# Attention and two MLPs in one kernel: TensorE's filler and score matmuls are queued behind the transposes of earlier slots

## The chip, the cores and the metric

The kernel runs on one core of one Trainium2 chip. The metric is the device time of one execution in microseconds (us); before the change the median of three runs is 1144.47 us (1142.77 to 1144.97).

## What is computed

Multi-head attention over 4 batches, 12 heads, 448 tokens and a head size of 64, with RMS-normalised queries and keys, and behind it two MLPs without biases:

```python
def _attn_ref(q, k, v, g_q, g_k):
    q_n, k_n = rmsnorm(q, g_q), rmsnorm(k, g_k)
    scores = scale * np.matmul(q_n, k_n.transpose(0, 1, 3, 2))
    scores = scores - np.max(scores, axis=-1, keepdims=True)
    attn = np.exp(scores)
    attn = attn / (np.sum(attn, axis=-1, keepdims=True) + 1e-09)
    return np.matmul(attn, v)

def _moe_ref(x, w1, w2, w3, w_out):        # 1792 tokens, 768 -> 1024 -> 768
    return ((x @ w1) * (x @ w2) @ w3) @ w_out

def _moe2_ref(x, w_in, w_out):             # 1792 tokens, 768 -> 2048 -> 768
    h = x @ w_in
    return (h * np.clip(h + 3.0, 0.0, 6.0) / 6.0) @ w_out
```

## The kernel before

**Stages.** The 48 heads are worked off as 24 pairs, numbered 0 to 23 here. A pair takes eight *slots*; a slot is one block of 112 queries of one head against all 448 keys. `attention` (L470) loops over the slots `t` (L875 to L902). While attention runs, TensorE also does *filler*: first the product of `w3` and `w_out` (`wprime`, L252), then layer 1 and layer 2 of the first MLP for the batches whose attention is finished (L391 and L396, L88 to L90). `fill` (L439) hands out some microseconds of filler per slot. When the slots are used up, at about 617 us, the rest of the filler runs alone; from about 705 us on the second MLP runs (L1242, L1304).

**One slot.** `score` (L618) makes the scores with two matmuls (L627, L628) into a bank of accumulator memory. VectorE scales them, finds the row maximum (L634) and negates it (L641); ScalarE takes the exponential (L646). Eight slots later `trans` (L649) turns the result in four small matmuls (L653). ScalarE copies the turned block out as `xh` (L662; for the block that two heads share L664 and L665), VectorE makes the remainder `xl` (L672; L674 and L675), and `pv` multiplies both with the values (L705 and L706; L696, L693 for the shared block). The turned blocks and the scores have two banks each.

**The round trip of a pair.** When the row sums of a pair are complete, TensorE turns them (L561; a second small one, L564, in every other pair), VectorE copies them (L578), one transfer takes them to DRAM (`rsd`), two bring them back spread over 64 partitions each (`rsb`), GpSimd multiplies the result of the pair with them (L730), and ScalarE splits that product for layer 1 (L359). I call the time from L561 to the end of L730 the round trip.

**What sets the order.** The kernel is written slot by slot, but a scheduler orders each engine's instructions when the program is built. `tc.issue_after(x)` around a block makes each instruction of that block that runs on `x`'s engine stand behind `x` in that engine's queue; it adds no wait at run time. Before the change the filler of slot `t` stands behind the scores, the maximum and the exponential of a slot two or three back (`anchors`, L897). At run time every engine works off its queue in order, and an instruction that waits holds up all that stands behind it.

Of the kernel before, what the change touches and what calls it, by code (L numbers as in the profile page):

```python
# [26 lines left out]
P = 128  # L27
CP = 112
# [22 lines left out]
def fused_kernel(ctx: ExitStack, tc: tile.TileContext, nat, qT, kT, vin, gq, gk,  # L51
                 w12, w3t, wo, win, wo2, outT):
    nc = tc.nc
# [16 lines left out]
    ident = cpool.tile([P, P], F32, name="ident")  # L70
# [21 lines left out]
    def bank(tag, name="bank"):  # L92
        return pp.tile([P, 512], F32, tag=tag, name=name)
# [12 lines left out]
    now = [0]  # L106
# [7 lines left out]
    def run_tasks():  # L114
        for fn, a in tasks.pop(now[0], ()):
            fn(*a)
# [322 lines left out]
    def fill(us, aux):  # L439

        state["aux"] = min(state["aux"] + aux, 2 * aux)
        while state["aux"] > 0 and prep[0] is not None:
            c = prep[0].step()
            if c is None:
                break
            state["aux"] -= c
        state["early"] = min(state["early"] + 0.6, 1.2)
        while state["early"] > 0 and "early" in L:
            c = next(L["early"], None)
            if c is None:  # L450
                break
            state["early"] -= c
        state["debt"] = min(state["debt"] + us, 2 * us)
        while state["debt"] > 0 and not state["done"]:
            try:
                c = next(filler)
            except StopIteration:
                state["done"] = True
                return
            if c is None:  # L460
                return
            state["debt"] -= c
            if "pool" in L:
                state["spent"] += c


    T = {}
    anchors = {}

    def attention(ap, rate):  # L470
        def full(i):
            return i in FULL
# [145 lines left out]
        def score(i, s):  # L618
            j, c = divmod(s, NC)
            if s == 0:  # L620
                T["PP", i] = ap.tile([CP, NC, 2 * S], F32, tag="PP", bufs=2, name="PP")
                T["m", i] = ap.tile([CP, 16], F32, tag="mx", bufs=2, name="mx")
                T["sum", i] = ap.tile([CP, 8], F32, tag="sum", bufs=2, name="sum")
            k1, k2 = T["K", i]
            ps = bank("s")
            qs = T["Q", i][:, j, c * CP : c * CP + CP]
            nc.tensor.matmul(ps[:CP, :S], qs, k1[:, j, :], start=True, stop=False)  # L627
            anchors[8 * i + s] = [nc.tensor.matmul(ps[:CP, :S], qs, k2[:, j, :], start=False, stop=True)]  # L628
            return ps

        def scale_max(i, s, ps):
            j, c = divmod(s, NC)
            sl = slice(j * S, j * S + S)
            anchors[8 * i + s].append(nc.vector.tensor_tensor_reduce(  # L634
                out=T["PP", i][:, c, sl], in0=ps[:CP, :S], in1=T["rb", i][:, sl],
                op0=ALU.mult, op1=ALU.max, scale=T["rq", i][:, s : s + 1], scalar=-3e38,
                accum_out=T["m", i][:, s : s + 1]))

        def negate(i, s):
            m = T["m", i]  # L640
            nc.vector.tensor_scalar_mul(m[:, 8 + s : 9 + s], m[:, s : s + 1], -1.0)  # L641

        def expo(i, s):
            j, c = divmod(s, NC)
            v = T["PP", i][:, c, j * S : j * S + S]
            anchors[8 * i + s].append(nc.scalar.activation(  # L646
                v, v, AF.Exp, bias=T["m", i][:, 8 + s : 9 + s], accum_out=T["sum", i][:, s : s + 1]))

        def trans(i, kb):  # L649
            src = T["PP", i]  # L650
            ps = bank("t")
            for c in range(NC):
                nc.tensor.transpose(ps[:, c * CP : c * CP + CP], src[:, c, kb * P : kb * P + P],  # L653
                                    ident[:CP, :CP])
            hi = ap.tile([P, S], F32 if full(i) else F32R, tag="xh", bufs=3, name="xh")
            lo = None if full(i) else ap.tile([P, S], F32R, tag="xl", bufs=3, name="xl")
            T["X", i, kb] = (ps[:, :S], hi, lo)

        def thi(i, kb):
            ps, hi, lo = T["X", i, kb]  # L660
            if kb != 3 or i < K3 or full(i):
                nc.scalar.activation(hi, ps, AF.Copy)  # L662
            else:
                nc.scalar.activation(hi[0:64, :], ps[0:64, :], AF.Copy)  # L664
                nc.scalar.activation(lo[64:128, :], ps[64:128, :], AF.Copy)  # L665

        def tlo(i, kb):
            ps, hi, lo = T["X", i, kb]
            if full(i):
                return  # L670
            if kb != 3 or i < K3:
                nc.vector.tensor_sub(lo, ps, hi)  # L672
            else:
                nc.vector.tensor_sub(hi[64:128, :], ps[0:64, :], hi[0:64, :])  # L674
                nc.vector.tensor_sub(lo[0:64, :], ps[64:128, :], lo[64:128, :])  # L675
# [57 lines left out]
        def xnext():  # L733
            for i in sorted(xs_ready)[: 2]:
                if len(L["xhl"]) < XB:
                    xsplit(i)
# [77 lines left out]
        ps = bank("t")  # L814
# [11 lines left out]
        for i in range(NP):  # L826
            t = 8 * i
# [46 lines left out]
        t = -1  # L874
        while t < 8 * NP + 23 or xs_ready:  # L875
            t += 1
            if t == 4:
                first.close()
            now[0] = t
            live = t < 8 * NP  # L880
            ps = score(*divmod(t, 8)) if live else None
            if 0 < t <= 8 * NP:
                expo(*divmod(t - 1, 8))
            u = t - LG
            if 0 <= u < 8 * NP and u % 8 < 7:
                trans(*divmod(u, 8))
            if 0 <= u - 1 < 8 * NP and (u - 1) % 8 < 7:
                tlo(*divmod(u - 1, 8))
            if live:
                scale_max(t // 8, t % 8, ps)  # L890
                negate(*divmod(t, 8))
            if 0 <= u < 8 * NP and u % 8 < 7:
                thi(*divmod(u, 8))
            if 0 <= u - 2 < 8 * NP and (u - 2) % 8 < 7:
                pv(*divmod(u - 2, 8))
            with ExitStack() as es:
                for a in anchors.get(t - (3 if "pool" in L else 2), ()):  # L897
                    es.enter_context(tc.issue_after(a.ins))
                fill(*rate(t))
            run_tasks()  # L900
            if "pool" in L:
                xnext()  # L902

    def rate(t):
        if "pool" not in L:
            return 1.3, 3
        if L["cur"] < 8:
            return 2.5, 4
        left = (B - 1) * (2 * M1 * KD * 3 + KD * M1 * 3) * 0.189 - state["spent"]
        return max(left - 25.0, 0.0) / max(8 * NP + 14 - t, 1), 2  # L910
# [508 lines left out]
```

## Time and profile before

| | |
|---|---|
| median of three runs | 1144.47 us (1142.77 to 1144.97) |
| the profiled execution's own time | 1141.81 us |
| its span, first to last instruction | 1140.0 us |
| TensorE busy | 1103.1 us, 97% of the span, 5483 matmuls |
| weight loads of TensorE | 944.0 us, 83% |
| VectorE busy | 850.8 us, 75% |
| ScalarE busy | 812.4 us, 71% |
| GpSimd busy | 177.9 us, 16% |
| DMA | 299.04 MB, mean 262 GB/s |
| granted TensorE clock, mean | 0.998 |

In the rows below PE is TensorE's matmuls, PEld its weight loads, DVE VectorE, ACT ScalarE, POOL GpSimd and SP the engine whose queue issues the transfers. Matmuls overlap: a matmul of 448 columns is shown as 0.36 us long, yet the next one starts 0.2 us after it. So idle time that stands in brackets on a PE row counts from the end of the drawn bar, and what was lost against back-to-back work is that figure and about 0.16 us more.

### The profile page before, as it was taken

Reading aid. Unit: us, or ns where it says so; the run is one execution under the profiler, and the core shown is the slowest. Engines: PE = TensorE matmul, PEld = TensorE weight load, DVE = VectorE, ACT = ScalarE, POOL = GpSimd, SP = SyncE. Lnnn points to the kernel's source line nnn. Section 1 sums busy time; section 2 is a strip of 40 time slices with the busy share of each in tenths; the row PEclk is TensorE's granted clock in tenths of the full one; section 3 lists DMA queues with packets and bytes.
Section 4 is the critical chain, followed back from the end, with each engine's and each line's share of the span. In section 5 each row is a group of like instructions: output and inputs, shape, how many; then the busy total and the mean of one; then the engine's idle time right before and its main releaser. Section 6 shows DMA issues by size and latency. Waiting matters only on the chain.

```text
span 1140.0 us, 17361 instructions
## 1 busy us (share of the span) xinstructions
PE 1103.1 (97%) x5483; PEld 944.0 (83%) x5483; DVE 850.8 (75%) x1927; ACT 812.4 (71%) x1729; POOL 177.9 (16%) x156
## 2 busy tenths in 40 slices
PE   5999999999999999999999999999999999999998
PEld 3545666788887888888888899899989989999998
DVE  5757988779866888778753225999988998887764
ACT  6989778899758878787754433766666776666764
POOL 1133223554322213221102000000000000000000
PEclk9999999999999999999999999999999999999999
DMA  8999655689889988997789998665469955434972
GB/s 267 331 317 342 213 171 164 243 293 377 272 279 316 308 295 269 336 342 253 232 287 324 382 362 299 217 214 200 164 228 362 389 172 168 153 117 160 335 264 74
DMA packets 109660, 299.04 MB, mean 262 GB/s; under 512 B 13280, under 2 KB 46048, under 8 KB 109568
## 3 DMA queue, kind: packets, MB, share of 16 engines
q1 hardware_dynamic: 109568, 297.93, 76.2%
q8 instruction: 43, 0.70, 0.3%
q14 instruction: 49, 0.40, 0.1%
HBM read 230.61 MB, written 67.27 MB: 261 GB/s over the span
## 4 chain that ended last, share of the span: by engine, by line
PE 60%; ACT 7%; DMA 7%; DVE 3%; issue 2%; POOL 0%; SPq 0%; ACTq 0%; POOLq 0%; DVEq 0%
PE acc L1304 17%; PE bank L391 10%; PE sB L1242 8%; PE sA L1242 8%; PE bank L396 5%; DMA rsb<-rsd 2%; PE bank L653 2%; ACT PP L646 1%; PE bank L88 1%; PE bank L89 1%; PE bank L90 1%; PE bank L627 1%; PE bank L628 1%; PE bank L706 1%; DMA raw<-in_wo_dram 1%
## 5 line engine op out<-in xcount | busy, mean ns | idle before, releaser
L1304 PE MATMUL acc<-g,wt 128*128 128x448 f32 x1008 | 211.7, 366 | 1.2 <-ACT g L1192 1.0
L1304 PEld LDWEIGHTS acc<-g,wt 128*128 128x128 f32 x1008 | 188.9, 188 | 17.7 <-ACT g L1192 1.9
L391 PE MATMUL bank<-xhl,ws 128*128 128x448 f32 x768 | 180.5, 367 | 1.6 <-ACT bs L367 1.3
L391 PEld LDWEIGHTS bank<-xhl,ws 128*128 128x128 f32 x768 | 143.5, 188 | 15.1 <-ACT bs L367 1.8
L634 DVE CUSTOM_DVE_ANT_0 PP<-bank,rb,rq 112x448 f32<-112x448 f32 x192 | 128.7, 675 | 27.4 <-PE bank L628 21.1
L646 ACT ACTIVATE PP<-PP,mx 112x448 f32<-112x448 f32 x192 | 127.5, 665 | 28.1 <-DVE mx L641 24.3
L1242 PE MATMUL sA<-xo,wt 128*128 128x448 f32 x504 | 112.0, 366 | 1.1 <-ACT u L1253 1.1
L1242 PE MATMUL sB<-xo,wt 128*128 128x448 f32 x504 | 112.2, 367 | 0.8 <-ACT u L1253 0.6
L252 PE MATMUL bank<-woh,w 128*128 128x384 f32 x256 | 97.6, 509 | 14.6 <-DVE woh L151 10.9
L1242 PEld LDWEIGHTS sB<-xo,wt 128*128 128x128 f32 x504 | 94.4, 188 | 9.9 <-ACT u L1253 1.9
L1242 PEld LDWEIGHTS sA<-xo,wt 128*128 128x128 f32 x504 | 94.6, 188 | 9.6 <-ACT u L1253 1.5
L662 ACT ACTIVATE xh<-bank 128x448 fp32r<-128x448 f32 (+1 forms) x156 | 83.1, 539 | 24.6 <-PE bank L653 20.5
L653 PEld LDWEIGHTS bank<-ident,PP 112*128 112x128 f32 x672 | 78.8, 141 | 23.9 <-issue 6.1
L1011 DVE TENSOR_TENSOR wt<-wf,wt 128x384 fp32r<-128x384 f32 x160 | 87.3, 555 | 15.1 <-ACT wt L1010 14.9
L672 DVE TENSOR_TENSOR xl<-bank,xh 128x448 fp32r<-128x448 f32 x142 | 87.4, 617 | 11.5 <-ACT xh L662 10.1
L653 PE MATMUL bank<-ident,PP 112*128 112x112 f32 x672 | 94.1, 261 | 1.5 <-DVE xl L672 1.1
L396 PE MATMUL bank<-xhl,ws 128*128 128x448 f32 x384 | 94.5, 366 | 0.0
L252 PEld LDWEIGHTS bank<-woh,w 128*128 128x128 f32 x256 | 48.9, 196 | 43.7 <-DVE woh L151 13.4
L148 ACT ACTIVATE raw<-raw 128x384 f32<-128x384 f32 (+1 forms) x112 | 63.8, 569 | 28.6 <-DMA raw<-in_wo_dram 11.6
L1010 ACT ACTIVATE wt<-wf 128x384 fp32r<-128x384 f32 x160 | 80.4, 517 | 4.8 <-PE acc L1304 2.7
L151 DVE SCALAR_TENSOR_TENSOR raw<-raw 128x384 int32<-128x384 int32 x80 | 48.9, 613 | 46.0 <-ACT raw L149 38.8
L627 PE MATMUL bank<-K,Q 128*112 128x448 f32 x192 | 77.7, 407 | 1.5 <-DVE mx L634 1.4
(134 smaller groups left out, 2110.3 us busy)
## 6 DMA issues: line engine op xcount, KB each, us to landing
ws<-w12d SPq DMA_DIRECT2D x48, 768.0 KB, 6.2
ws<-wpd SPq DMA_DIRECT2D x32, 768.0 KB, 6.5
wf<-wfd SPq DMA_DIRECT2D x56, 384.0 KB, 5.6
raw<-in_wo_dram SPq DMA_DIRECT2D x44, 384.0 KB, 5.8
td<-G SPq DMA_DIRECT2D x32, 448.0 KB, 2.5
G<-td SPq DMA_DIRECT2D x32, 448.0 KB, 6.2
raw<-in_w_dram SPq DMA_DIRECT2D x32, 384.0 KB, 6.9
w12d<-ws SPq DMA_DIRECT2D x16, 768.0 KB, 5.9
```

The costliest lines, as they stand in the source:

```text
L252: nc.tensor.matmul(ps[:, :NH], W["w3"][a, c // 4][:, cs], W["woh"][c, n], start=c == 0, stop=c == M1 - 1)
L391: nc.tensor.matmul(ps[:, :S], w[:, 0, ks], x[:, y, :], start=k == 0 and y == 0, stop=False)
L396: nc.tensor.matmul(ps[:, :S], w[:, 1, ks], L["xhl"][i][:, 0, :], start=False, stop=k == KD - 1)
L627: nc.tensor.matmul(ps[:CP, :S], qs, k1[:, j, :], start=True, stop=False)
L634: anchors[8 * i + s].append(nc.vector.tensor_tensor_reduce(out=T["PP", i][:, c, sl], in0=ps[:CP, :S], in1=T["rb", i][:, sl], op0=ALU.mult, ...
L646: anchors[8 * i + s].append(nc.scalar.activation(v, v, AF.Exp, bias=T["m", i][:, 8 + s : 9 + s], accum_out=T["sum", i][:, s : s + 1]))
L653: nc.tensor.transpose(ps[:, c * CP : c * CP + CP], src[:, c, kb * P : kb * P + P], ident[:CP, :CP])
L662: nc.scalar.activation(hi, ps, AF.Copy)
L672: nc.vector.tensor_sub(lo, ps, hi)
L1011: nc.vector.tensor_sub(t[:, 1, :], src, t[:, 0, :])
L1242: mm = nc.tensor.matmul(ps[:, :S], w[:, a, ks], x[:, c, :], start=first and k == 0 and n == 0, stop=k == KD // 2 - 1 and n == 2, skip_grou ...
L1304: nc.tensor.matmul(ps, w[:, y, ns], x[:, z, :], start=first and a == 0, stop=end and a == 2, skip_group_check=h in "674")
```

## The change

`trans` notes the last transpose that it issues in a slot. The scores of slot `t` are then issued behind the transposes of slot `t - 3`, and the filler of slot `t`, beside its old anchors, behind the transposes of slot `t - 2`.

```diff
     anchors = {}
+    turned = {}
...
             for c in range(NC):
-                nc.tensor.transpose(ps[:, c * CP : c * CP + CP], src[:, c, kb * P : kb * P + P],
-                                    ident[:CP, :CP])
+                turned[now[0]] = nc.tensor.transpose(ps[:, c * CP : c * CP + CP], src[:, c, kb * P : kb * P + P],
+                                                     ident[:CP, :CP])
...
-            ps = score(*divmod(t, 8)) if live else None
+            with tc.issue_after(turned[t - 3].ins) if t - 3 in turned else ExitStack():
+                ps = score(*divmod(t, 8)) if live else None
...
                 for a in anchors.get(t - (3 if "pool" in L else 2), ()):
                     es.enter_context(tc.issue_after(a.ins))
+                if t - 2 in turned:
+                    es.enter_context(tc.issue_after(turned[t - 2].ins))
                 fill(*rate(t))
```

Every engine has the same instructions before and after, the transfers included; only their order differs. Line numbers of the changed file are one higher from L469 to L881, so its L654 is L653 here. Three places follow.

TensorE where the sums of pair 18 are turned (487 to 491.5 us in the trace of before). L653 are transposes of the next pair's blocks, L696, L705 and L706 their products with the values, L88 to L90 filler. Before:

```order
L90 MATMUL bank<-abh,ws 128x448
L696 MATMUL bank<-xh,vo 128x448
L653 MATMUL bank<-ident,PP 128x112 x4
L696 MATMUL bank<-xl,vo 128x448
L705 MATMUL bank<-xh,vo 128x448
L653 MATMUL bank<-ident,PP 128x112 x4
L706 MATMUL bank<-xl,vo 128x448
L705 MATMUL bank<-xh,vo 128x448
L561 MATMUL bank<-ident,sum 8x112
L706 MATMUL bank<-xl,vo 128x448
L653 MATMUL bank<-ident,PP 128x112 x4
L705 MATMUL bank<-xh,vo 128x448
```

The change, from the same sums on (L562 here is L561 there):

```order
L562 MATMUL bank<-ident,sum 8x112
L88 MATMUL bank<-abh,ws 128x448
L89 MATMUL bank<-abh,ws 128x448
L707 MATMUL bank<-xl,vo 128x448
L654 MATMUL bank<-ident,PP 128x112 x4
L706 MATMUL bank<-xh,vo 128x448
L90 MATMUL bank<-abh,ws 128x448
L628 MATMUL bank<-K,Q 112x448
L629 MATMUL bank<-K,Q 112x448
L88 MATMUL bank<-abh,ws 128x448
L707 MATMUL bank<-xl,vo 128x448
L654 MATMUL bank<-ident,PP 128x112 x4
```

Three groups of transposes with no filler between them stood here; now filler and scores stand between one group and the next, and a product stands further behind the transposes that it needs. Counted over the part from 200 us on, 17 of the 99 products L705 and L696 stood six or fewer wide matmuls (448 columns) behind the transposes that they depend on, 16 of them three; in the change the smallest such distance is 18.

ScalarE around the split L359 of pair 10 (L646 is an exponential, L148 and L149 convert raw weights, L662 copies a turned block out, L526 and L527 belong to the normalisation). Before:

```order
L646 ACTIVATE PP,sum<-PP,mx 112x448
L527 ACTIVATE ry<-ry 112x32
L359 ACTIVATE xhl<-xs 128x448
L646 ACTIVATE PP,sum<-PP,mx 112x448
L148 ACTIVATE raw<-raw 128x384
L149 ACTIVATE raw<-raw 128x384
L662 ACTIVATE xh<-bank 128x448
```

The change:

```order
L412 ACTIVATE bs<-bank 128x448
L663 ACTIVATE xh<-bank 128x448
L359 ACTIVATE xhl<-xs 128x448
L647 ACTIVATE PP,sum<-PP,mx 112x448
L148 ACTIVATE raw<-raw 128x384
L149 ACTIVATE raw<-raw 128x384
L663 ACTIVATE xh<-bank 128x448
```

What stands on ScalarE between the split and the next copy is the same. On TensorE, from the pair's L561 to the first matmul that reads that copy, there stood 72 wide and 17 small matmuls; now there are 55 wide and 17 small. The same count at other pairs: pair 11 (to the first L696) 87 wide and 17 small before, 69 and 17 now; pair 17 now 68 and 25; pair 18 now 70 and 25.

ScalarE around the split of pair 23, the last one (L412 empties a layer-2 bank, and the filler two groups on needs that bank). Before:

```order
L713 ACTIVATE xs<-bank 64x448
L412 ACTIVATE bs<-bank 128x448
L359 ACTIVATE xhl<-xs 128x448
L412 ACTIVATE bs<-bank 128x448 x2
```

The change:

```order
L372 ACTIVATE abh<-bs 128x448
L359 ACTIVATE xhl<-xs 128x448
L148 ACTIVATE raw<-raw 128x384
L149 ACTIVATE raw<-raw 128x384
L412 ACTIVATE bs<-bank 128x448
```

A conversion pair has come between the split and L412. On TensorE, from the L561 of pair 23 to the filler that needs the bank, there stood 86 wide matmuls; now there are 79. After the last transposes 613 filler matmuls are left instead of 540.

## Rows read from the trace of the kernel before

**Rows 1.** The page, part 1: busy time and share of the span.
```profile
PE 1103.1 (97%) x5483; PEld 944.0 (83%) x5483; DVE 850.8 (75%) x1927; ACT 812.4 (71%) x1729; POOL 177.9 (16%) x156
```

**Rows 2.** Stages, all engines: stretch, its length, then busy us (instructions); clock, DMA last.
```profile
200.00:600.00 400.00, 391.48 (x2117) 343.98 (x2117) 310.47 (x797) 316.60 (x707) 116.70 (x99) 1.00 0.87 293
...
705.00:1140.00 435.00, 428.32 (x2097) 392.69 (x2095) 359.39 (x683) 288.21 (x593) 0.00 (x0) 1.00 0.61 216
```

**Rows 3.** TensorE's waits, 50 to 705 us: total us, times, longest us.
```profile
PE bank L705 <- ACT xh L662: 3.8, 6, 1.3
PE bank L696 <- DVE xh L674: 2.4, 1, 2.4
...
PE bank L653 <- DVE xl L672: 1.1, 5, 0.3
PE bank L706 <- DVE mx L641: 0.6, 1, 0.6
```

**Rows 4.** Timeline of TensorE, 405 to 412 us: start, length, what, [idle before].
```profile
405.97 1.81 PE L391 MATMUL bank<-xhl,ws 128*128 128x448 f32 x8
...
411.90 0.55 PE L653 MATMUL bank<-ident,PP 112*128 112x112 f32 x4
```

**Rows 5.** Timeline, all engines, 328 to 350 us: the round trip of pair 11.
```profile
328.03 0.26 PE L564 MATMUL bank<-ident,rr 112*16 112x112 f32 x1
...
341.09 1.16 POOL L730 TENSOR_TENSOR xs<-xs,rsb 128x448 f32<-128x448 f32 x1 [5.87 <-DMA rsb<-rsd]
...
342.28 0.58 ACT L359 ACTIVATE xhl<-xs 128x448 fp32r<-128x448 f32 x1 [5.56 <-POOL xs L730]
342.76 0.66 ACT L646 ACTIVATE PP<-PP,mx 112x448 f32<-112x448 f32 x1
...
343.42 1.04 ACT L510 ACTIVATE nat<-nat 112x1024 f32<-112x1024 f32 x1
...
349.41 0.62 DVE L674 TENSOR_TENSOR xh<-bank,xh 64x448 fp32r<-64x448 f32 x1 [2.13 <-ACT xl L665]
...
350.09 0.48 PE L696 MATMUL bank<-xh,vo 128*128 128x448 f32 x1 [2.40 <-DVE xh L674]
```

**Rows 6.** Stages, behind that wait: columns as in rows 2.
```profile
350.50:353.50 3.00, 2.73 (x12) 2.49 (x12) 1.84 (x6) 2.18 (x7) 0.00 (x0) 0.50 1.03 407
```

**Rows 7.** Timeline, TensorE and GpSimd, pairs 17 and 18: turned sums, product, waits.
```profile
466.80 0.26 PE L564 MATMUL bank<-ident,rr 112*16 112x112 f32 x1
...
481.81 1.15 POOL L730 TENSOR_TENSOR xs<-xs,rsb 128x448 f32<-128x448 f32 x1 [6.22 <-DVE mx L634]
...
488.62 0.47 PE L705 MATMUL bank<-xh,vo 128*128 128x448 f32 x1 [0.29 <-ACT xh L662]
...
490.84 0.47 PE L705 MATMUL bank<-xh,vo 128*128 128x448 f32 x1 [0.74 <-ACT xh L662]
...
513.78 0.47 PE L705 MATMUL bank<-xh,vo 128*128 128x448 f32 x1 [0.85 <-ACT xh L662]
```

**Rows 8.** Timeline, TensorE and ScalarE, pair 10: turned sums to the first reader.
```profile
304.96 0.26 PE L561 MATMUL bank<-ident,sum 112*8 112x112 f32 x1
...
319.89 0.54 ACT L148 ACTIVATE raw<-raw 128x384 f32<-128x384 f32 x1
320.33 0.54 ACT L149 ACTIVATE raw<-raw 128x384 int32<-128x384 uint16 x1
320.77 0.53 ACT L662 ACTIVATE xh<-bank 128x448 fp32r<-128x448 f32 x1
...
321.38 0.47 PE L693 MATMUL bank<-xh,vo 64*128 64x448 f32 x2
```

**Rows 9.** Timeline, TensorE and GpSimd: the round trips of pairs 20 and 23.
```profile
537.66 0.26 PE L561 MATMUL bank<-ident,sum 112*8 112x112 f32 x1
...
546.03 1.58 POOL L730 TENSOR_TENSOR xs<-xs,rsb 128x448 f32<-128x448 f32 x1
...
609.31 0.26 PE L561 MATMUL bank<-ident,sum 112*8 112x112 f32 x1
...
625.77 1.15 POOL L730 TENSOR_TENSOR xs<-xs,rsb 128x448 f32<-128x448 f32 x1 [20.43 <-DMA rsb<-rsd]
...
628.02 0.47 PE L88 MATMUL bank<-abh,ws 128*128 128x448 f32 x1 [0.79 <-ACT bs L412]
```

## The prediction

> **What bounds the kernel.** I read the page's busy shares first: TensorE's matmuls fill 97% of the span [rows 1]. Then the stages: in the attention stretch from 200 to 600 us TensorE is drawn busy for 391.48 of 400 us, VectorE for 78%, ScalarE for 79%, and the granted clock is 1.00 [rows 2]. TensorE is the bound, and the second MLP from 705 us on, which the change does not touch, has it busy for 428.32 of 435 us. As the change removes and adds no instruction, it can save only what TensorE waits, and cost only new waits. So the next view is TensorE's waits, and the last one the timeline around each long wait, to see what comes late.
>
> Two kinds are to be seen there. The first I call **crowding**: a product L705 stands so close behind the transposes that it depends on that ScalarE has not yet copied the block out, or transposes want a bank that VectorE has not yet emptied. The second is the **round trip**: ScalarE stands at the split L359 until a pair's turned sums have been through DRAM and back, 5.56 us in one case [rows 5]; every copy queued behind the split comes late, and TensorE waits for one of them.
>
> **The units.** Eight back-to-back filler matmuls take 1.81 us drawn, the last of them 0.37 alone, so one follows the other after (1.81 - 0.37) / 7 = 0.206 us; four transposes take 0.55 us, the last 0.26, so 0.097 us each [rows 4]. A drawn wait is therefore short by about 0.37 - 0.206 = 0.16 us, and I add 0.17 for every wait.
>
> **What there is to gain.** The waits on a transposed block or its bank, from 50 to 705 us, are 3.8 + 2.4 + 1.1 + 0.6 = 7.9 us in 13 waits [rows 3]; with 13 x 0.17 that is 10.1 us. The single longest one, 2.40 + 0.17 = 2.6 us, belongs to the round trip of pair 11 [rows 5]. Three waits of 0.29, 0.74 and 0.85 us, 2.4 us with their supplements, follow the round trips of pairs 17 and 18, where a late ScalarE meets crowded transposes [rows 7]. The rest, 10.1 - 2.6 - 2.4 = 5.1 us in nine waits, is crowding alone.
>
> **The change, part by part.**
>
> *Crowding.* In the new order no product stands fewer than 18 wide matmuls behind its transposes, 18 x 0.206 = 3.7 us; a copy takes 0.53 us [rows 8]. With 3.7 us of cover ScalarE can be three microseconds behind and nobody waits. I let the 5.1 us go. What covers them is filler that was used elsewhere before: the transposes end earlier, and 73 more filler matmuls run after them, which costs nothing as they are back to back there too.
>
> *Pairs 17 and 18.* For pair 17 the turned sums start at 466.80 us and L730 ends at 481.81 + 1.15 = 482.96, a trip of 16.2 us [rows 7]. Now only the split and one copy follow on ScalarE, 0.58 + 0.53 us [rows 5, 8], so the copy is there after 17.3 us. TensorE has 68 x 0.206 + 25 x 0.097 = 16.4 us of work up to its reader: a wait of 0.9 us. Pair 18 has two wide matmuls more and, with the same trip, waits 0.5. From 2.4 to 1.4 us: a gain of 1.0.
>
> *Pair 11.* Before, the work up to the reader was 87 x 0.206 + 17 x 0.097 = 19.6 us, while the matmul started 350.09 - 328.03 = 22.1 us after the sums: 2.5 us late, and the row says 2.6 [rows 5]. The method holds there. Now the cover is 69 x 0.206 + 17 x 0.097 = 15.9 us. The trip is 341.09 + 1.16 - 328.03 = 14.2 us; behind it come the split (0.58), one evacuation L412 and the copies L664 and L665 (0.53 each, as L662), an exponential (0.66), the squares (1.04) and VectorE's part (0.62): 4.5 us [rows 5, 8]. 18.7 against 15.9 is a wait of 2.8. I count 0.2 us of loss.
>
> *Pair 10.* Before, it was just in time: the reader L693 started 321.38 - 304.96 = 16.4 us after the sums, 0.08 us after the copy had ended, and its cover was 72 x 0.206 + 17 x 0.097 = 16.5 us [rows 8]. The instructions on ScalarE between split and copy are the same now, but the cover is 55 x 0.206 + 17 x 0.097 = 13.0 us. That is a new wait of 3.4 us. Queued behind the waiting product are scores and filler, so all of TensorE stands.
>
> *Pair 23.* Before, the filler L88 waited 0.79 + 0.17 = 1.0 us for its bank, 628.02 - 609.31 = 18.7 us after the sums [rows 9]. Now a conversion pair stands in between, 320.77 - 319.89 = 0.9 us [rows 8], and the cover is 79 x 0.206 + 0.1 = 16.4 us. With the same trip the wait would be 18.7 + 0.9 - 16.4 = 3.2 us. But this trip of 625.77 + 1.15 - 609.31 = 17.6 us is long; pair 20 needed 546.03 + 1.58 - 537.66 = 10.0 us [rows 9], with which nothing would wait. Between 0 and 3.2 us I take 1.0, as before, since the trip moves by some 15 us (73 x 0.206) to another place among the transfers; the ends make -1.0 and +2.2 us.
>
> *The transfers.* All transfers stay, in a partly different order on SP; I have no row for their new times. Bounded by the trips of 10.0 and 17.6 us, each of the waits above could be nothing or up to some 3 us longer. I keep the trips of before.
>
> *The clock.* Behind the 2.40 us wait the granted clock was 0.50 for the next 3 us [rows 6], the 1.2 GHz level: half of that, 1.5 us, was lost. One such wait, at pair 11, stays; pair 10's may bring a second. I put 0 for the second and keep 1.5 us as its upper end.
>
> **Sum.** -5.1 - 1.0 + 0.2 + 3.4 + 0 = -2.5 us. Against the profiled execution's 1141.81 us that is 1139.3; its median stands 2.66 us higher, so 1144.47 - 2.5 = 1142.0 us.
>
> **Rivals.**
>
> *The round trips also shorten* (0.15). In the new order SP has fewer transfers between the sums and their return at pair 10. Against it: the return can't start before the sums have landed. If the waits of pairs 10, 11, 17, 18 and 23 vanish as well, the gain is 5.1 + 2.4 + 2.6 + 1.0 and the 1.5 us of slow clock, 12.6 us; half way between forecast and that end it is about 7.5 us: 1137.0.
>
> *The round trip takes the place of the crowding and costs more* (0.28, slower). Its place is the split L359 of pairs 10, 11, 17, 18 and 23. For it speaks that the distance from the sums to the first reader has shrunk by 17 to 20 wide matmuls, 3.5 to 4.1 us, at pairs 10, 11, 17 and 18 alike. The price is one for one: each microsecond by which the five trips are longer costs 5 us, and a slow stretch of 1.5 us follows the waits at pair 10 and pair 23. It decides from trips that are 0.5 us longer: -2.5 + 2.5 = 0. With 1 us longer and both slow stretches it is -2.5 + 5 + 3 = +5.5 us: 1150.0.
>
> *The waits change places* (0.20, no difference). ScalarE is 79% busy in this stretch and works in bursts; the copies wait there instead of at the end of a crowd, and -5.1 becomes about -2.5: 1144.5, give or take 2.
>
> *A ceiling* (0.01). The weight loads take 343.98 of 400 us in the attention stretch, 86.0%, and 392.69 of 435 us, 90.3%, in the second MLP [rows 2]. If the new order lets attention reach that share, it needs 343.98 / 0.903 = 380.9 us, 19.1 us less, and the time is 1125.4. Against it: the waits in the rows come to 10.1 us only. The Trainium skill (Perfetto Trace Analysis, section Identifying the Most-Contended Engine) holds that the busy share of matmuls is no good measure of TensorE's headroom and that of its weight loads is; by it all of the 19.1 us would be headroom, and nothing in this trace shows more than the 10.1.
>
> **How the numbers follow.** The forecast, 1142.0, has a chance of 0.36 and a range of its own from 1139 to 1144.5. A measurement of this kernel tells some 0.2%, 2.3 us, from no change: below 1142.2 counts as faster, above 1146.8 as slower. Faster: 0.15 + 0.01 and 0.25 of the forecast's 0.36 make 0.41. The same: 0.11 of it and 0.19 of the third rival, 0.30. Slower: 0.28 and 0.01, 0.29. For eight times in ten I leave out the better half of the first rival, below 1135.5, and the upper third of the second, above 1150.5.
>
> **What would show it.** Right: TensorE's waits on L662 fall from 3.8 us to under 1; a wait of about 3 us appears some 13 us after the sums of pair 10, released by ScalarE's copy, with L359 idle before it; pair 11 keeps its wait and its slow stretch. The prediction fails if L705 still waits in many small pieces (then crowding was not the cause), or if pair 10 shows no wait (then the trip is shorter than I took it), or if the granted clock falls in several places.

## The result, and the profile after

The changed kernel takes 1154.26 us in the median of six runs (1151.83 to 1158.19), the kernel before 1144.79 us beside it: a ratio of 1.0088, 95% interval 1.0062 to 1.0114. It is slower, and outside the predicted range. The profiled execution took 1156.66 us, its span is 1154.9 us, 14.9 us more than before. The page's busy shares, which answer to [rows 1]:

```profile
PE 1107.7 (96%) x5483; PEld 947.8 (82%) x5483; DVE 852.0 (74%) x1927; ACT 813.5 (70%) x1729; POOL 175.9 (15%) x156
```

The stages, columns as in [rows 2]; first the changed kernel:

```profile
50.00:200.00 150.00, 140.84 (x606) 88.53 (x605) 109.33 (x296) 122.39 (x269) 43.79 (x38) 0.99 0.74 239
200.00:300.00 100.00, 94.20 (x493) 80.01 (x492) 82.71 (x200) 87.53 (x200) 47.68 (x42) 0.98 0.84 287
200.00:600.00 400.00, 386.47 (x2091) 339.58 (x2090) 312.47 (x808) 317.72 (x711) 117.67 (x101) 0.99 0.87 288
705.00:1140.00 435.00, 432.09 (x2111) 395.66 (x2110) 367.21 (x697) 289.68 (x595) 0.00 (x0) 1.00 0.63 224
```

and the kernel before in the first two of these stretches:

```profile
50.00:200.00 150.00, 145.29 (x635) 93.33 (x634) 114.61 (x313) 126.87 (x281) 46.33 (x41) 1.00 0.76 246
200.00:300.00 100.00, 97.75 (x521) 84.02 (x521) 81.73 (x199) 89.27 (x201) 50.30 (x44) 1.00 0.87 302
```

Between 50 and 300 us TensorE gets 29 + 28 matmuls less done. The second MLP starts 14.1 us later (its first L1246 at 735.2 us, L1242 at 721.1 us before), so nearly all of the 14.9 us is lost ahead of it; it stands shifted in the window from 705 us, whose busy times can't be compared as they are. TensorE's waits from 50 to 705 us, which answer to [rows 3], add up to 25.2 us in 25, where they were 14.1 us in 24:

```profile
PE bank L697 <- DVE xh L675: 5.2, 2, 2.8
PE bank L654 <- DVE mx L642: 4.3, 4, 1.6
PE bank L654 <- DVE xl L673: 3.1, 5, 0.9
PE bank L706 <- ACT xh L663: 3.1, 3, 1.2
PE bank L252 <- DVE wst L245: 2.5, 1, 2.5
...
PE bank L628 <- DVE mx L635: 1.4, 3, 0.9
PE bank L706 <- DVE rss L579: 1.3, 1, 1.3
PE bank L707 <- DVE mx L642: 1.2, 1, 1.2
```

The kind has changed. Products waited for ScalarE's copy before; now it is mostly transposes (L654), scores (L628) and products of the shared block (L697) that wait for VectorE. Between 50 and 300 us alone VectorE releases 13.2 us of waits against 3.8 before, 6.2 us against 0.7 of them at transposes. One of them in the timeline of all engines, 123 to 126 us:

```profile
123.16 2.65 POOL L609 TENSOR_TENSOR K<-kr,K 128x448 fp32r<-128x448 f32 x2
...
123.54 1.26 DVE L601 SCALAR_TENSOR_TENSOR Q<-qr,gs,Q 64x448 fp32r<-64x448 f32 x1
...
123.95 0.37 PE L629 MATMUL bank<-K,Q 128*112 128x448 f32 x1
124.28 0.54 ACT L663 ACTIVATE xh<-bank 128x448 fp32r<-128x448 f32 x1
...
124.83 0.62 DVE L673 TENSOR_TENSOR xl<-bank,xh 128x448 fp32r<-128x448 f32 x1
...
125.38 0.14 DVE L642 TENSOR_SCALAR mx<-mx 112x1 f32<-112x1 f32 x1
...
125.52 0.47 PE L707 MATMUL bank<-xl,vo 128*128 128x448 f32 x1 [1.19 <-DVE mx L642]
125.83 0.55 PE L654 MATMUL bank<-ident,PP 112*128 112x112 f32 x4
```

The profile names L642, which came last, but what L707 reads is `xl`, ready at 124.83 + 0.62 = 125.45 us. L673 stood behind L601, the remainder of the queries, and that took 1.26 us. The copy L663 in these lines is a later block's: copies and remainders follow one another in the same order, 142 of each, and by that count L673 works on the copy that ended at 121.78 us.

The granted clock was 0.50, the 1.2 GHz level, in one stretch inside the kernel before [rows 6]. Now it is so in five:

```profile
70.00:73.00 3.00, 3.00 (x6) 1.66 (x5) 2.49 (x7) 3.00 (x7) 0.90 (x2) 0.50 0.88 267
206.50:209.50 3.00, 3.00 (x11) 2.25 (x11) 2.87 (x7) 2.08 (x5) 0.99 (x1) 0.50 0.83 274
353.30:356.30 3.00, 3.00 (x10) 2.65 (x9) 2.71 (x9) 2.95 (x7) 2.15 (x2) 0.50 0.68 266
462.50:465.50 3.00, 3.00 (x10) 2.59 (x9) 2.77 (x8) 2.95 (x10) 0.12 (x1) 0.50 1.05 349
606.00:609.00 3.00, 3.00 (x10) 2.70 (x9) 2.02 (x4) 2.60 (x6) 0.00 (x0) 0.50 1.01 372
```

Each lasts 3.4 us and follows a wait of 1.2 to 2.8 us. At half the clock 1.7 us of it are lost, so four more cost about 4 x 1.7 = 6.8 us, an estimate; with 11.1 us more of waits that is 17.9, more than the 14.9 us, and why is open: no wait of over 0.15 us lies inside one of the five stretches. By the pages' own sums TensorE is drawn busy 4.6 us longer (1107.7 against 1103.1) and idle 10.3 us longer.

Two of the five stretches belong to this execution alone. The waits ahead of them, 2.51 us at L252 (69.16 us) and 2.38 us at L697 (604.72 us), begin where ScalarE stands at the conversion of raw weights whose transfer has not landed; at the second place:

```profile
602.07 0.54 ACT L148 ACTIVATE raw<-raw 128x384 f32<-128x384 f32 x1 [3.16 <-DMA raw<-in_wo_dram]
...
604.72 0.47 PE L697 MATMUL bank<-xh,vo 128*128 128x448 f32 x1 [2.38 <-DVE xh L675]
```

A second execution of the changed kernel (below) has neither wait.

The later places, which answer to [rows 5, 7, 8]: the first readers of pairs 10 and 11, then two products, the second behind the round trip of pair 17:

```profile
324.19 0.47 PE L694 MATMUL bank<-xh,vo 64*128 64x448 f32 x2 [0.15 <-ACT xh L663]
...
351.78 0.47 PE L697 MATMUL bank<-xh,vo 128*128 128x448 f32 x1 [2.82 <-DVE xh L675]
...
460.42 0.47 PE L706 MATMUL bank<-xh,vo 128*128 128x448 f32 x1 [1.20 <-ACT xh L663]
...
494.38 0.47 PE L706 MATMUL bank<-xh,vo 128*128 128x448 f32 x1 [1.25 <-ACT xh L663]
```

### The profile page after: what moved, and what is told of

Read it like the earlier page. It is cut to its first block, busy times and chain, and to the rows that moved or that the text cites. A ratio compares the mean times of both kernels' runs of the same rounds, so it can differ in the third digit from the quotient of the medians.

```text
span 1154.9 us, 17361 instructions
## 1 busy us (share of the span) xinstructions
PE 1107.7 (96%) x5483; PEld 947.8 (82%) x5483; DVE 852.0 (74%) x1927; ACT 813.5 (70%) x1729; POOL 175.9 (15%) x156
## 4 chain that ended last, share of the span: by engine, by line
PE 73%; DMA 9%; DVE 7%; ACT 7%; issue 2%; SPq 0%; POOL 0%; ACTq 0%; DVEq 0%; POOLq 0%
PE acc L1308 17%; PE bank L391 10%; PE sB L1246 8%; PE sA L1246 8%; PE bank L252 6%; PE bank L396 5%; PE bank L654 4%; DMA nat<-in_nat_dram 3%; PE bank L628 2%; PE bank L88 2%; PE bank L89 2%; PE bank L90 2%; PE bank L629 2%; DVE PP L635 2%; DMA rsb<-rsd 1%
## 5 line engine op out<-in xcount | busy, mean ns | idle before, releaser
L391 PE MATMUL bank<-xhl,ws 128*128 128x448 f32 x768 | 184.2, 371 | 2.3 <-ACT bs L367 1.5
L252 PE MATMUL bank<-woh,w 128*128 128x384 f32 x256 | 100.3, 524 | 15.8 <-DVE woh L151 11.1
L1246 PE MATMUL sA<-xo,wt 128*128 128x448 f32 x504 | 112.1, 366 | 1.1 <-ACT u L1257 1.1
L1246 PE MATMUL sB<-xo,wt 128*128 128x448 f32 x504 | 112.3, 367 | 0.7 <-ACT u L1257 0.6
L673 DVE TENSOR_TENSOR xl<-bank,xh 128x448 fp32r<-128x448 f32 x142 | 87.4, 617 | 23.6 <-ACT xh L663 22.6
L654 PEld LDWEIGHTS bank<-ident,PP 112*128 112x128 f32 x672 | 78.3, 141 | 31.5 <-issue 10.2
L1246 PEld LDWEIGHTS sB<-xo,wt 128*128 128x128 f32 x504 | 94.4, 188 | 9.9 <-ACT u L1257 1.8
L654 PE MATMUL bank<-ident,PP 112*128 112x112 f32 x672 | 94.5, 262 | 8.3 <-DVE mx L642 4.3
L1246 PEld LDWEIGHTS sA<-xo,wt 128*128 128x128 f32 x504 | 94.6, 188 | 9.6 <-ACT u L1257 1.5
L663 ACT ACTIVATE xh<-bank 128x448 fp32r<-128x448 f32 (+1 forms) x156 | 83.3, 537 | 19.1 <-PE bank L654 16.9
L396 PE MATMUL bank<-xhl,ws 128*128 128x448 f32 x384 | 94.8, 369 | 0.0
L252 PEld LDWEIGHTS bank<-woh,w 128*128 128x128 f32 x256 | 48.8, 201 | 46.0 <-DVE woh L151 13.6
L148 ACT ACTIVATE raw<-raw 128x384 f32<-128x384 f32 (+1 forms) x112 | 64.0, 571 | 26.5 <-DMA raw<-in_w3t_dram 8.0
L628 PE MATMUL bank<-K,Q 128*112 128x448 f32 x192 | 79.3, 415 | 2.2 <-DVE mx L635 2.2
L151 DVE SCALAR_TENSOR_TENSOR raw<-raw 128x384 int32<-128x384 int32 x80 | 50.7, 635 | 40.1 <-ACT raw L149 37.4
```

The source lines that it names most:

```text
L252: nc.tensor.matmul(ps[:, :NH], W["w3"][a, c // 4][:, cs], W["woh"][c, n], start=c == 0, stop=c == M1 - 1)
L391: nc.tensor.matmul(ps[:, :S], w[:, 0, ks], x[:, y, :], start=k == 0 and y == 0, stop=False)
L396: nc.tensor.matmul(ps[:, :S], w[:, 1, ks], L["xhl"][i][:, 0, :], start=False, stop=k == KD - 1)
L654: turned[now[0]] = nc.tensor.transpose(ps[:, c * CP : c * CP + CP], src[:, c, kb * P : kb * P + P], ident[:CP, :CP])
L1246: mm = nc.tensor.matmul(ps[:, :S], w[:, a, ks], x[:, c, :], start=first and k == 0 and n == 0, stop=k == KD // 2 - 1 and n == 2, skip_grou ...
```

## The experiments

Ratios are to the kernel before on the same chip, five rounds, with 95% intervals. "The early stage" is the part in which `w'` is multiplied, up to about 200 us.

**Which rule.** One of the two `with` blocks of the change is left out.

> Only the filler's rule is kept (filler of slot t behind the transposes of slot t - 2); the scores stand where the scheduler puts them. Theory A (early stage: while w' is multiplied, up to about 200 us, VectorE and ScalarE are the late ones, and whoever is tied behind the transposes waits for them): this half carries most of the loss, 1150 to 1155 us, waits of TensorE from 50 to 300 us of 10 us or more, and at least two stretches of granted clock 0.50. Theory B (round trip: ScalarE stands at the split L359 of later pairs, now under a shorter cover): the filler's rule alone moves the 73 filler matmuls behind the last transposes, as in the change, so also about 1152 us, but with the waits from 300 us on, at L697/L706, and few ones before. It is the place of the waits that tells them apart.

> Only the scores' rule is kept (scores of slot t behind the transposes of slot t - 3); the filler is anchored as before. Theory A: less than half of the loss, 1145 to 1148 us; the early waits stay near the 4.3 us that the kernel before has from 50 to 200 us. Theory B: 24 filler matmuls more than before stand behind the last transposes, a third of the change's 73, so a third of the loss, about 1148 us, with the waits from 300 us on. If neither holds and the scores' rule is the bad half, 1152 us or more, with waits of the scores and of transposes for VectorE's maxima (L634/L641).

Measured: the filler's rule 1.0019 (0.9993 to 1.0045), the scores' rule 1.0022 (0.9995 to 1.0049). Neither half alone is told from no change, and they don't add up to 1.0088: it takes both. That the filler's rule would carry most of the loss, as theory A had it, did not come. The waits that VectorE releases between 50 and 300 us are 11.0 and 7.6 us. With the filler's rule 6.2 us of these stand at transposes, with the scores' rule 1.0. The 6.2 us are as many as in the change, and yet the filler's rule loses 0.2% only. So the waits in one trace do not give the time by themselves.

**Which stage.**

```diff
-            with tc.issue_after(turned[t - 3].ins) if t - 3 in turned else ExitStack():
+            with tc.issue_after(turned[t - 3].ins) if t - 3 in turned and "pool" in L else ExitStack():
...
-                if t - 2 in turned:
+                if t - 2 in turned and "pool" in L:
```

That is late rules alone (`"pool" in L` is true from the end of `w'` on); for early rules alone it is `not in`.

> Both rules, but only from the end of w' on (about 200 us); before that the order is that of the kernel before. Theory A: the loss is gone, and what the prediction had worked out for the later pairs is left, crowding away and the wait at pair 11 kept: 1140 to 1146 us, waits from 50 to 200 us about 4 us. Theory B: the loss stays, 1151 us or more, with waits and slow stretches from 200 us on as in the change.

> Both rules, but only up to the end of w' (about 200 us); from then on the filler is anchored as before. Theory A: the loss stays, 1151 us or more, with 9 us or more of waits between 50 and 200 us and a slow stretch of the clock near 70 us. Theory B: as fast as the kernel before within 2 us, 1143 to 1147 us.

Measured: late 0.9973 (0.9947 to 0.9999), early 1.0060 (1.0037 to 1.0083). TensorE's order is that of the kernel before up to 196 us in the first, and that of the change up to 209 us in the second. This settles the place: the loss needs the rules in the early stage, and most of it is there with these alone. Theory A holds as to the place, theory B does not. The parts don't add, though: 0.9973 x 1.0060 is 1.0033, not 1.0088. Together with the early rules the late ones show no gain. TensorE's waits at transposes and scores, 50 to 300 us, with late rules alone:

```profile
PE bank L654 <- DVE mx L642: 0.8, 1, 0.8
...
PE bank L628 <- DVE mx L635: 0.3, 1, 0.3
PE bank L654 <- DVE xl L673: 0.2, 1, 0.2
```

and with early rules alone:

```profile
PE bank L654 <- DVE mx L642: 3.0, 3, 1.6
PE bank L628 <- DVE mx L635: 2.7, 5, 0.9
PE bank L654 <- DVE xl L673: 1.7, 2, 1.0
```

**The changed kernel again, and the split L359 issued later.** In the second and third kernel the split L359 is to be issued four slots later, so that ScalarE should not stand at it; `since[i]` is the slot in which the program issues the pair's product.

```diff
-                if len(L["xhl"]) < XB:
+                if len(L["xhl"]) < XB and now[0] >= since[i] + 4:
```

> The changed kernel once more, beside the other runs of this chip. Both theories: 1.0062 to 1.0114 times the kernel before. It is also the yardstick for the next two runs, and it shows which waits of TensorE come again and which belong to one execution: theory A expects 9 us or more of waits between 50 and 200 us again.

> The change, with the split L359 of a pair issued four slots later, so that ScalarE does not stand at it while a pair's sums are under way. Theory A (the loss lies in the early stage, before the first split): the wait of about 2.8 us at pair 11 goes, with its slow stretch of 1.7 us, 2 to 5 us off the change, so still 1.003 or more times the kernel before. Theory B (the round trip is the loss): back to the kernel before or faster, a ratio of 1.000 or less.

> Both rules only after w' (as in the run with late rules alone, ratio 0.9973) and the split L359 four slots later: the wait of 2.76 us at pair 11 with its slow stretch of 1.7 us, and parts of the wait of 2.24 us at pair 18, should go. Theory A: 2 to 5 us less than late rules alone, a ratio of 0.993 to 0.996. If the later split only moves the waits (the split waits for nothing any more, but layer 1 of a pair comes later), 0.997 as before.

Measured: the change 1.0098 (1.0076 to 1.0121), with the later split 1.0091 (1.0071 to 1.0112). The edit did not do what it was made for. ScalarE still stands at the split of pair 11, and the wait at that pair's product is still there (L360 and L698 are L359 and L697 of the change):

```profile
345.01 0.58 ACT L360 ACTIVATE xhl<-xs 128x448 fp32r<-128x448 f32 x1 [3.17 <-POOL xs L732]
...
349.31 0.74 PE L698 MATMUL bank<-xh,vo 128*128 128x448 f32 x1 [2.81 <-DVE xh L676]
```

So this run says nothing on the round trip. That the round trip is not the main loss rests on the early rules alone, which lose 0.6% with the later order not tied. Together with the late rules the edit changed nothing at all: every engine has the same instructions in the same order as with late rules alone. That run, 0.9994 (0.9972 to 1.0017), is a second measurement of late rules alone; with 0.9973 before it, a gain of theirs is not shown.

In the second execution of the change most of the early waits are at the same instructions as in the first, and transposes again wait 6.2 us for VectorE up to 300 us; between 50 and 200 us, however, all waits come to 5.5 us, not the 9 that I expected. VectorE releases 9.5 us of waits between 50 and 300 us there, and the waits from 50 to 705 us come to 19.1 us; it has six slow stretches.

**Filler tied to the scores instead.**

```diff
-                if t - 2 in turned:
+                if t - 2 in turned and "pool" in L:
                     es.enter_context(tc.issue_after(turned[t - 2].ins))
+                if "pool" not in L and t - 1 in anchors:
+                    es.enter_context(tc.issue_after(anchors[t - 1][0].ins))
```

> The change, but up to the end of w' the filler of slot t stands behind the scores of slot t - 1 instead of behind the transposes of slot t - 2; the scores' rule stays, and later both rules. In the program, transposes with no filler between them and the scores before them fall from 37 of 53 groups to 10 of 52 in that stage (13 of 51 in the kernel before). Theory A1 (such transposes want a bank that VectorE empties only after it has worked off those scores, so filler must lie between): about as fast as with late rules alone, 1142 to 1149 us, and the waits between 50 and 200 us back at 4 to 6 us. If any tie of the filler in that stage costs (A2, less room for the scheduler), 1151 us or more.

Measured: 1.0063 (1.0041 to 1.0085). Theory A1 falls. The waits at transposes are gone (0.9 us), but products and scores now wait for VectorE in their place:

```profile
PE bank L707 <- DVE xl L673: 2.9, 2, 1.5
PE bank L706 <- DVE rss L579: 2.4, 2, 2.0
PE bank L628 <- DVE mx L635: 2.3, 4, 0.8
```

Theory A2, that any tie of the filler in that stage costs, fits the time, 1153.88 us. It is not which neighbour the transposes have: with a tie of either kind TensorE waits for VectorE's results somewhere.

**ScalarE or VectorE relieved.** Two edits, each made to the change and to the kernel before. ScalarE is relieved of two copies a pair, VectorE of L601; GpSimd does both instead.

```diff
-            nc.scalar.activation(k1, r, AF.Copy)
+            nc.gpsimd.tensor_copy(k1, r)
...
-            nc.scalar.activation(vo[:, :, :, 0, :], r, AF.Copy)
+            nc.gpsimd.tensor_copy(vo[:, :, :, 0, :], r)
```

```diff
-                nc.vector.scalar_tensor_tensor(out=q, in0=T["qr", i][a, j, :], scalar=G[a, :], in1=q,
-                                               op0=ALU.mult, op1=ALU.subtract)
+                r = T["qr", i][a, j, :]
+                nc.gpsimd.tensor_scalar_mul(r, r, G[a, :])
+                nc.gpsimd.tensor_sub(q, r, q)
```

> The change with ScalarE relieved: the first halves of the splits of keys and values (k1, vo; 0.96 and 0.63 us per pair on ScalarE) are copied by GpSimd. Theory A3 (the loss comes where weights are converted, 50 to 120 us and 200 to 300 us, since ScalarE is 91% and 89% busy there and has no slack when TensorE's order brings a burst): about half of the loss goes, a ratio of 1.002 to 1.006, and less than 9 us of TensorE's waits between 50 and 300 us (changed kernel: 18.9 and 13.4 us in two executions). Theory A4 (it is VectorE that is late, ScalarE only follows): 1.007 or more, as the change.

> The kernel before with ScalarE relieved in the same way, to tell what the relief is worth by itself. Theory A3: less than with the change, a ratio of 0.997 to 1.000, because before the change ScalarE's lateness meets more slack on TensorE. If the relief is worth the same here as with the change (0.995 or less), the two have nothing to do with each other.

> The change with VectorE relieved: the remainder of the queries (L601, twice per pair, 0.68 to 1.47 us each) is made by GpSimd in two steps. Theory A4 (the transposes wait for a bank behind L601 on VectorE): about half of the loss goes, 1.002 to 1.006, and the waits at the transposes near 126 and 266 us, which follow a long L601, vanish. Theory A3: 1.007 or more.

> The kernel before with VectorE relieved in the same way. Theory A4: less than with the change, 0.997 to 1.001. If it gains as much as there, the relief says nothing about the change. GpSimd takes about 4 us more per pair; if the round trips get longer by that, 1.001 to 1.004.

> The change with both reliefs, L601 and the first halves of the splits on GpSimd. Theory A4 (VectorE's lateness is the change's loss): with that gone the relief of ScalarE is worth what it is worth before the change, 0.989 to 0.994. If GpSimd, then busy for some 45% between 50 and 300 us, is late itself or lengthens VectorE's other instructions, 0.996 or more.

> The kernel before with both reliefs, the control of the run of the change with both (0.9931). Theory A4 (the change costs where VectorE is late; with VectorE relieved the new order is the better one): slower than that run, 0.994 to 0.999. If the change costs something of its own whatever VectorE does, faster than it, 0.984 to 0.990.

| edit | kernel before with it | change with it | the change's own worth |
|---|---|---|---|
| none | 1 | 1.0088, 1.0098 | 1.009 |
| ScalarE relieved | 0.9933 (0.9906 to 0.9960) | 0.9994 (0.9964 to 1.0023) | 1.006 |
| VectorE relieved | 1.0030 (1.0002 to 1.0059) | 0.9984 (0.9953 to 1.0015) | 0.995 |
| both | 0.9918 (0.9887 to 0.9950) | 0.9931 (0.9911 to 0.9952) | 1.001 |

The last column is the third over the second; by the two intervals it is good to about 0.004. ScalarE's relief is worth some 0.7% to 0.9% either way: no tie to the change is shown, and theory A3 falls, as its 1.002 to 1.006 and 0.997 to 1.000 were both missed; so was theory A4's 1.007 for the first. TensorE's waits between 50 and 300 us, 14.7 and 11.0 us in the two executions of the change (the expectation's 18.9 and 13.4 us are not what the view of waits gives), are 9.9 us with ScalarE relieved, 9.6 of them at VectorE. With L601 off VectorE the change costs nothing, once 0.5% less and once 0.1% more than the kernel before with the same edit. Theory A4 expected that, but the pairs do not prove it, for three reasons. The scheduler sets every engine anew for the edited program: in the change with VectorE relieved TensorE's own order differs from 26.6 us on, and some 690 of its 5483 matmuls stand elsewhere in the sequence. The kernel before with the edit gets slower, 1.0030 instead of theory A4's 0.997 to 1.001, and there products wait 7.3 us in five for ScalarE's copies between 50 and 300 us; part of the 0.995 is this. And with both reliefs VectorE still releases 6.9 us of waits in the change against 2.9 in the kernel before, and the two take the same time. Theory A4's last step, that the new order would then be the better one, does not hold either. What TensorE waits for VectorE at transposes, 50 to 300 us, in the change with VectorE relieved (4.0 us against 6.2):

```profile
PE bank L655 <- DVE mx L643: 2.2, 2, 1.2
...
PE bank L655 <- DVE xl L674: 1.8, 2, 1.1
```

**Does L601 make VectorE late?** Its median is 0.685 us, its maximum 1.5. The wait at 268.95 us in the trace of the change:

```profile
266.30 1.30 POOL L617 TENSOR_TENSOR vo<-vr,vo 128x512 fp32r<-128x512 f32 x1 [1.49 <-ACT vo L616]
...
266.65 1.43 DVE L601 SCALAR_TENSOR_TENSOR Q<-qr,gs,Q 64x448 fp32r<-64x448 f32 x1
...
268.23 0.57 DVE L673 TENSOR_TENSOR xl<-bank,xh 128x448 fp32r<-128x448 f32 x1
...
268.95 0.58 PE L654 MATMUL bank<-ident,PP 112*128 112x112 f32 x4 [1.31 <-DVE mx L642]
```

L601 is long where GpSimd is already making a remainder when it starts. It does not account for most of the waits: of the 13 that VectorE releases between 50 and 300 us, 13.2 us, four stand behind a long L601 (at 125.52, 190.64, 205.81 and 268.95 us, 4.5 us), others behind a long conversion of weights, L151 (1.55 us at 105.60 us, median 0.56). And a long one need not cost: the kernel before has three, of 1.50 to 1.58 us (at 99.53, 120.12 and 255.32 us), and the longest wait of TensorE within 3 us of their ends is 0.58 us. I moved the split of the values four slots, so that L617 should not meet it.

```diff
-SHIFT = {'ssum': -1, 'vsplit': -2, 'load_v': 2, 'rsum1': -1, 'rms1': 0}
+SHIFT = {'ssum': -1, 'vsplit': 2, 'load_v': 2, 'rsum1': -1, 'rms1': 0}
```

> The change, with the split of the values (vsplit: L616 on ScalarE and L617, its remainder, on GpSimd) four slots later, so that L617 no longer runs while VectorE makes the remainder of the queries (L601). Theory A5 (the long L601 is what makes VectorE late): L601 takes 0.68 us at those places, the waits of 0.70, 1.28 and 1.31 us near 190, 206 and 269 us go with two slow stretches of the clock, some 7 us, a ratio of 1.002 to 1.005. If the length of L601 does not matter, 1.008 to 1.010 as the change.

> The kernel before with the split of the values four slots later. Control of the run above: there L617 lengthens one L600 (at 99 us, 1.59 instead of 0.68 us) and no wait of TensorE over 0.3 us follows, so theory A5 expects 0.998 to 1.001. If it gains as much as the run above, the later split is worth something by itself and says nothing on the change.

Measured: the change 1.0045 (1.0030 to 1.0060), the kernel before 0.9952 (0.9935 to 0.9969). The first is inside the range that theory A5 gave, but the edit gains the same in both, and theory A5 expected nothing in the kernel before; so it says nothing on the change, whose own worth stays 1.009. Nor did it take all meetings away. In the changed kernel with it, at two places:

```profile
123.24 2.65 POOL L609 TENSOR_TENSOR K<-kr,K 128x448 fp32r<-128x448 f32 x2
123.36 1.52 DVE L601 SCALAR_TENSOR_TENSOR Q<-qr,gs,Q 64x448 fp32r<-64x448 f32 x1
125.59 0.47 PE L707 MATMUL bank<-xl,vo 128*128 128x448 f32 x1 [1.25 <-DVE mx L642]
...
203.90 0.68 DVE L601 SCALAR_TENSOR_TENSOR Q<-qr,gs,Q 64x448 fp32r<-64x448 f32 x1
```

At the first, L609 still lengthens L601 and the wait is there; at the second L601 is short, and the wait behind it fell from 1.28 to 0.50 us. So whether it is L601's length or its mere place before `xl` that costs is not settled by this.

**A better version.** Edits that gained, put together: late rules with ScalarE relieved, and the kernel before with ScalarE relieved and the later split of the values.

> Both rules only after w', and the first halves of the splits of keys and values copied by GpSimd. If the two gains add (0.9973 and 0.9933), 0.989 to 0.992; if the relief of ScalarE already removes what the late rules remove (waits for ScalarE's copies L662), 0.993 to 0.996.

> The kernel before with the first halves of the splits on GpSimd (0.9933 by itself) and the split of the values four slots later (0.9952 by itself). If the two add, 0.986 to 0.990; if both remove the same waits, 0.993.

Measured: 0.9952 (0.9937 to 0.9967) and 0.9926 (0.9900 to 0.9952). The gains don't add; behind ScalarE's relief the late rules gain nothing. Four kernels lie at 0.992 to 0.993 and can't be told apart; all beat both kernels, and the simplest of them is the kernel before with ScalarE's two copies on GpSimd.

## Why the prediction was wrong

**Crowding: the step "I let the 5.1 us go".** It counted distances only from 200 us on, and only from transposes to products. In place of a gain of 5.1 us TensorE's waits for VectorE from 50 to 300 us rose from 3.8 to 13.2 us, in the second execution to 9.5. That the rules in the early stage make the loss is shown by the two kernels with the rules in one stage. That it goes through VectorE is read from the waits and not shown: the pairs of kernels with L601 elsewhere change TensorE's order too. That the ties move transposes and scores closer to VectorE's results in a stage where a slot has less filler is my explanation; no run tests it, and what exactly the early ties cost stays open.

The part about ScalarE came true only in small part: waits for its copies at L705 fell from 3.8 us in six [rows 3] to 3.1 us in three, where I had asked for under 1. The 3.7 us of cover did not let ScalarE be three microseconds behind without a wait. It stood 3.15 us at the squares L511 for a transfer, ahead of the 1.20 us wait at 460.42 us, which comes again in the second execution (1.30 us at 457.09 us):

```profile
456.54 1.06 ACT L511 ACTIVATE nat<-nat 112x1024 f32<-112x1024 f32 x1 [3.15 <-DMA nat<-in_nat_dram]
```

I had written of crowding as two kinds, a copy not made and a bank not emptied, and then priced the cover for the first alone.

**The clock: "I put 0 for the second".** Four more slow stretches came in the profiled execution, about 6.8 us. Over all runs it is less: beside the second measurement of the change the mean granted clock is 0.9925 in its six runs and 0.9963 in eighteen of the kernel before, by which some 0.0038 x 1150 = 4.4 us of the 11.1 us between their medians are clock, an estimate. I had named "the granted clock falls in several places" as a sign of failure, and it was one.

**Pair 10: a new wait of 3.4 us.** It was 0.15 us. The cover did shrink, but the trip did too: its sums start at 310.93 us and the product L731 ends at 320.42 + 1.16 us, 10.7 us. Before, the product ended at 317.57 + 1.15 us, a trip of 13.8 us, and I kept the trips of before. The 3.1 us between them is nearly the whole 3.4. First the kernel before, then the change:

```profile
317.57 1.15 POOL L730 TENSOR_TENSOR xs<-xs,rsb 128x448 f32<-128x448 f32 x1 [7.19 <-DMA rsb<-rsd]
...
310.93 0.26 PE L562 MATMUL bank<-ident,sum 112*8 112x112 f32 x1
...
320.42 1.16 POOL L731 TENSOR_TENSOR xs<-xs,rsb 128x448 f32<-128x448 f32 x1 [6.37 <-DMA rsb<-rsd]
```

**Pair 11: 2.8 us.** It was 2.82 us, with its slow stretch; the method holds where the trip stays (14.4 us against 14.2). The close number is luck in part: in the second execution the same wait is 1.27 us.

**Pairs 17 and 18: 2.4 to 1.4 us.** Behind their sums stand waits of 1.25 and 0.62 us, 2.2 us with supplements. Only the first follows a split (of pair 17, trip 16.5 us); the second, at 512.46 us, comes before the split of pair 18 begins at 516.72 us. **Pair 23:** no wait at all, a gain of 1.0 us; in the second execution it was 1.58 us (L88, at 621.19 us).

**The rivals.** The one on the slower side had the sign but not the mechanism: its place was the split L359 from pair 10 on, and the loss is there with the rules in the early stage alone. From 300 to 705 us, where those pairs lie, all waits of TensorE rose from 7.4 us to 10.5, in the second execution to 8.0. The third rival, waits that change places, came nearest, but named ScalarE and put the price at half of the gain, where the waits came at VectorE, most of them in another stage, and the loss was several times the gain.

Late rules alone, at 0.9973, gain 0.0027 x 1144.47 = 3.1 us (0.1 to 6.1), near the 2.5 us that the prediction had worked out for the part it looked at. I don't count that as a confirmation: the same program measured 0.9994 on another chip, from 300 us on that kernel's trace shows no less waiting than before, and the terms of the sum don't reappear one by one.

## What to carry to other kernels

An order rule that acts on the whole loop must be counted in each stage of it, above all where a slot has the least filler, and in all directions: product behind copy, transposes behind an emptied bank, scores behind the maxima. Filler placed by a tie covers one dependence and uncovers another; look which engine the next result comes from, and whether that engine keeps up in that stage. And where an engine in between is late in bursts, taking an instruction off it may be worth more than the order: the edit that relieves ScalarE gained 0.7% in the kernel before. Before an edit is counted as a test, look in the trace whether it changed what it was to change, and what else it moved.

## What the runs showed of the hardware

VectorE's L601 takes 0.68 us by itself, and up to 1.50 us when GpSimd is at a remainder as it starts (L609 and L617, but also L227, L340 and L360): so nine of 48 in the trace of the change, four of 48 in the kernel before. In all nine it ended 0.48 to 0.49 us after GpSimd's instruction (the one at 203.55 us took 1.27 us, L601 from 203.84 us on 1.47). Where L601 started first it kept its 0.68 us (at 104.88 us, GpSimd's L617 from 105.37 us on). L673, one of whose inputs lies in a bank, kept its 0.57 to 0.63 us beside GpSimd's work. The Trainium skill (SBUF — State Buffer, section Who interferes with whom) says that a VectorE instruction with two inputs in SBUF contends with a GpSimd instruction that reads SBUF, that the shared ports are an exclusive lock, and that issue order decides who blocks. The trace agrees as to which instruction is lengthened; as L601 ends within less than its usual 0.68 us after GpSimd's end, GpSimd's drawn span or the block is not exact.

A stretch of 3.4 us at the lower clock level followed waits as short as 1.28 us here (at 205.81 us), and in one case waits of 1.20 and 0.87 us (at 460.42 and 461.76 us), not only the 2.40 us wait before [rows 6]. The kernel before has waits of 1.50, 1.30 and 1.28 us with no such stretch behind them, so the length of one wait alone does not tell.
